# Three sums over partitions: one f32 product with ones, or two fp32r products of a high and a low part

## The chip, the core and the metric

The kernel runs on one core of one Trainium2 chip. The metric is the device time of one execution in microseconds (us), as the median of several runs. An execution is also recorded by the hardware profiler; the engines in the record are PE (TensorE matmuls), PEld (TensorE weight loads), DVE (VectorE), ACT (ScalarE), POOL (GpSimd) and SP (SyncE, which issues all DMAs here). L464 is line 464 of the kernel's file.

## The reference

One transformer block on 2048 tokens of width 512, all in f32. A vector `c` modulates it: six vectors of 512 come out of `silu(c) @ w_mod` and shift, scale and gate two branches.

```python
mod = (_silu(c) @ w_mod).reshape(c.shape[0], 6, 1, -1)
sa, ca, ga, sb, cb, gb = (mod[:, 0], mod[:, 1], mod[:, 2], mod[:, 3], mod[:, 4], mod[:, 5])
h = _layernorm(x, axis=-1) * (1 + ca) + sa
x = x + ga * _A_ref(h, A_wqkv, A_wo)
h = _layernorm(x, axis=-1) * (1 + cb) + sb
x = x + gb * _B_ref(h, B_w_gate, B_w_up, B_w_down)
```

`_A_ref` is linear attention with 32 heads of 16. With phi(t) = (t + 1 where t > 0, else exp(t)) + 1e-6 it takes `kv = sum over tokens of phi(k) v`, `z = sum over tokens of phi(k)`, and `o = phi(q) kv / (phi(q) z + 1e-6)`, and multiplies by `wo`. `_B_ref` is `((x w_gate) * (x w_up)) w_down`.

The change concerns three sums over the 128 partitions: the gates `ga` (vector 2) and `gb` (vector 5) of `mod`, and `z`.

## The kernel before, in words

**Order.** The order of the work is written out by hand (`tc.manual_schedule()`): each engine executes its instructions in the order in which the source issues them, and waits on semaphores for its operands. All working tiles of 128x512 come from one pool of 99 buffers (tag `"t"`); a new tile waits until the last reader of its buffer is done. Products write into PSUM banks: four `bank()`s that are taken in turn, and four `acc_bank()`s.

**Products in parts.** Nearly all matmuls use operands that are split into a high part of type fp32r and a low part that holds the rest. `split` does this: a copy to fp32r on ACT (L183) and a subtraction on DVE (L184), which needs the copy. `product` (L196 to L198) then issues three matmuls: high by high, high by low, low by high.

**The token loop.** The first part of the kernel goes over 16 token tiles of 128 tokens (`for i in range(NT)`). In tile i the source issues, in this order:

1. `proj(i + 2, wk)`, twelve matmuls (L196 to L198) of the normalised tokens by the key weights; in the last tiles the query projections of tiles 4 and 5 instead, of which tile 15 issues that of tile 5.
2. `k_split_x(i + 1)` and `k_split(i + 1)`: the parts of the tokens and of phi(k) for the next tile, on ACT (L183, L318) and DVE (L184, L319).
3. `k_phi`, or in the last tiles `q_a` and `q_b`: two ACT instructions (L291, L292), then one on DVE (L295) that needs them.
4. `z_add(i + 1)`: phi(k) of the next tile added into `zacc` on DVE (L312). After tile 14's, `zacc` holds 128 partial sums per column, one in each partition.
5. In tile 15 only: the product of `zacc` with a 128x128 tile of ones (L464), which sums over the partitions and gives every partition the result, and its copy `zb` on ACT (L466).
6. `t_tile(i, ...)`: twelve matmuls (L327 to L329) that add tokens by phi(k) into the four banks `tacc`.
7. `extra[i]`, a table of side work. Its entries that bear on the change: tile 9 ends the weighted sum `accs[2]` of the four row blocks of `w_mod` (`mod_part(2, 2, 3)`, DVE, L161); tile 11 issues `mod_row(2, accs[2])`; tile 14 issues the last part of `accs[5]` (`mod_part(5, 3)`) and splits the four tiles of `wo` (`wo_s`, four ACT copies L183 and four DVE subtractions L184); tile 15 issues `mod_row(5, accs[5])`.

`mod_row` sums over partitions in the same way as step 5: one f32 product with `ones` (L176) and a copy on ACT (L178).

**After the loop.** `den_z` reduces `zb` on DVE (L480, L481), and `den_a(0, 0, 1)` multiplies and reduces twice (L486, L492, L486, L492). Query projections of tiles 6 and 7 run on PE. `tacc` is scaled on ACT (L535) and shifted by `zb` on DVE (L536), four tiles; these are split (L183 on ACT, L184 on DVE, four each) into `tt`. Then `kvps` is built: for each of four column groups, `product` over k = 0 to 3 of the parts of `wv[k]` and of `tt[k]`, 128x128 matmuls at L196 to L198. The first group already takes all four `tt[k]`, and the second matmul of each three takes the low part of `tt[k]`.

The second half of the kernel (attention output, second norm, and the gated feed-forward in a form with fewer block products, L837 and L916 to L918) is untouched.

## Time and profile before

| | us |
|---|---|
| median of 3 runs | 572.92 (571.94 to 573.11) |
| span of the profiled execution | 570.9 |
| PE busy | 560.6 (98%) |
| PEld busy | 457.3 (80%) |
| DVE busy | 373.8 (65%) |
| ACT busy | 279.7 (49%) |
| POOL busy | 185.6 (33%) |

The span runs from the first to the last recorded instruction of one execution; the runs' times take in what lies around it, 2.0 us between this span and the median. In the timeline view a row gives start, duration, engine, line, operation, tiles and shapes; "x4" means that four instructions of a kind were merged into one row, and a bracket gives the idle time of the engine just ahead and what ended it. An f32 matmul of 128x512 shows as two PE records ("x2"). Ends of matmuls are modelled by the profiler, so PE is read from starts.

### The profile page before, as it was taken

How to read it: one execution, taken by the hardware profiler on the slowest of the kernel's cores; microseconds unless marked ns; L12 is line 12 of the kernel's file. 1: busy time of each engine (PE TensorE's matmuls, PEld its weight loads, DVE VectorE, ACT ScalarE, POOL GpSimd, SP SyncE). 2: the span in 40 equal slices, each digit the busy share in tenths (PEclk: the TensorE clock that was granted, in tenths of full speed). 3: DMA queues.
4: the chain of work that ended last, by engine and by line, in shares of the span. 5: the costliest groups of instructions: out<-in, count | busy, mean ns of one | idle time of the engine just before them, and what ended most of it. 6: DMA issues, size and time to landing. Idle time of an engine off the chain costs nothing.

```text
span 570.9 us, 7343 instructions
## 1 busy us (share of the span) xinstructions
PE 560.6 (98%) x2569; PEld 457.3 (80%) x2569; DVE 373.8 (65%) x613; ACT 279.7 (49%) x500; POOL 185.6 (33%) x191
## 2 busy tenths in 40 slices
PE   7999999999999999999989999999999999999997
PEld 6778888888888778878878888887888888888885
DVE  6876868868768876768776777755554434344444
ACT  3785857546456535445865545533333333334110
POOL 2000000000011300000389666665667446556200
PEclk9999999999999999999999999999999999999999
DMA  8900223302301000804208462699436122100004
GB/s 279 378 6 2 73 75 102 121 0 57 96 0 52 24 1 37 258 0 136 68 2 276 147 209 93 218 337 335 126 110 174 29 56 55 57 18 2 0 1 147
DMA packets 50165, 59.34 MB, mean 104 GB/s; under 512 B 6416, under 2 KB 26896, under 8 KB 50128
## 3 DMA queue, kind: packets, MB, share of 16 engines
q1 hardware_dynamic: 50128, 58.87, 32.0%
q8 instruction: 20, 0.33, 0.2%
q14 instruction: 17, 0.14, 0.1%
HBM read 43.12 MB, written 15.73 MB: 103 GB/s over the span
## 4 chain that ended last, share of the span: by engine, by line
PE 88%; DVE 4%; ACT 2%; DMA 2%; POOL 2%; issue 1%; SPq 0%; POOLq 0%; DVEq 0%; ACTq 0%
PE bank L837 28%; PE acc L614 7%; PE acc L916 6%; PE acc L917 6%; PE acc L918 6%; PE bank L198 5%; PE bank L196 5%; PE bank L197 5%; PE acc L329 3%; PE acc L328 3%; PE acc L327 3%; PE bank L691 2%; PE bank L692 2%; PE bank L690 2%; PE bank L250 1%; PE bank L578 1%
## 5 line engine op out<-in xcount | busy, mean ns | idle before, releaser
L837 PE MATMUL bank<-h,w 128*128 128x512 f32 (+1 forms) x798 | 185.3, 390 | 1.6 <-DVE u L892 1.6
L837 PEld LDWEIGHTS bank<-h,w 128*128 128x128 f32 (+1 forms) x798 | 148.2, 186 | 34.9 <-DVE u L892 2.5
L842 ACT ACTIVATE bank<-bank 128x512 f32<-128x512 f32 (+1 forms) x38 | 22.2, 583 | 144.7 <-PE bank L837 144.7
L677 DVE TENSOR_TENSOR x<-acc,x 128x512 f32<-128x512 f32 x72 | 48.9, 690 | 49.2 <-PE acc L918 48.5
L823 POOL TENSOR_TENSOR w<-raw,w 128x256 fp32r<-128x256 f32 (+3 forms) x38 | 42.2, 1111 | 97.0 <-ACT w L816 76.7
L184 POOL TENSOR_TENSOR w<-raw,w 128x512 fp32r<-128x512 f32 (+1 forms) x25 | 35.5, 1422 | 115.9 <-DVE mv L226 87.5
L916 PE MATMUL acc<-w,kh 128*128 128x512 f32 (+1 forms) x152 | 59.2, 390 | 0.0
L917 PE MATMUL acc<-w,kh 128*128 128x512 f32 (+1 forms) x152 | 59.2, 390 | 0.0
L918 PE MATMUL acc<-w,kl 128*128 128x512 f32 (+1 forms) x152 | 59.1, 389 | 0.0
L234 POOL TENSOR_TENSOR rstd<-ve,half 128x4 f32<-128x4 f32 (+1 forms) x9 | 9.4, 1045 | 138.2 <-DVE ve L233 136.6
L184 DVE TENSOR_TENSOR kl<-u,kh 128x512 fp32r<-128x512 f32 (+1 forms) x38 | 27.4, 761 | 34.5 <-ACT kh L183 32.6
L823 POOL TENSOR_TENSOR w<-t,w 128x512 fp32r<-128x512 f32 (+1 forms) x38 | 48.0, 1286 | 0.0
L196 PE MATMUL bank<-w,h 128*128 128x512 f32 x112 | 44.9, 401 | 0.0
L198 PE MATMUL bank<-w,h 128*128 128x512 f32 x112 | 43.9, 392 | 0.0
L197 PE MATMUL bank<-w,h 128*128 128x512 f32 x112 | 43.6, 389 | 0.0
L614 PE MATMUL acc<-w,xh 128*128 128x512 f32 x120 | 38.1, 398 | 0.0
L916 PEld LDWEIGHTS acc<-w,kh 128*128 128x128 f32 (+1 forms) x152 | 28.5, 188 | 6.0
L918 PEld LDWEIGHTS acc<-w,kl 128*128 128x128 f32 (+1 forms) x152 | 28.5, 188 | 6.0
L917 PEld LDWEIGHTS acc<-w,kh 128*128 128x128 f32 (+1 forms) x152 | 28.5, 188 | 6.0
L243 ACT ACTIVATE n<-x,nmr,rstd 128x512 f32<-128x512 f32 x32 | 24.1, 805 | 17.2 <-DVE nmr L237 17.2
L892 DVE TENSOR_TENSOR u<-bank,u 128x512 f32<-128x512 f32 (+1 forms) x19 | 13.1, 691 | 28.8 <-PE bank L837 28.8
L183 ACT ACTIVATE w<-raw 128x512 fp32r<-128x512 f32 (+2 forms) x44 | 26.4, 618 | 3.2 <-DMA raw<-in_A_wqkv_dram 2.2
(177 smaller groups left out, 1098.1 us busy)
## 6 DMA issues: line engine op xcount, KB each, us to landing
raw<-in_w_mod_dram SPq DMA_DIRECT2D x24, 256.0 KB, 3.7
raw<-in_B_w_down_dram SPq DMA_DIRECT2D x20, 256.0 KB, 3.0
raw<-in_B_w_gate_dram SPq DMA_DIRECT2D x36, 128.0 KB, 3.5
raw<-in_B_w_up_dram SPq DMA_DIRECT2D x36, 128.0 KB, 3.6
x<-in_A_x_dram SPq DMA_DIRECT2D x16, 256.0 KB, 5.4
kept<-f SPq DMA_DIRECT2D x16, 256.0 KB, 2.1
f<-kept SPq DMA_DIRECT2D x16, 256.0 KB, 4.6
side_s<-h SPq DMA_DIRECT2D x16, 256.0 KB, 2.9
```

The costliest lines, as they stand in the source:

```text
L183: nc.scalar.activation(h, src, AF.Copy)
L184: (low or nc.vector).tensor_tensor(l, src, f32(h), op=ALU.subtract)
L196: nc.tensor.matmul(ps, ah, bh, start=i == 0, stop=False)
L197: nc.tensor.matmul(ps, ah, bl, start=False, stop=False)
L198: nc.tensor.matmul(ps, al, bh, start=False, stop=i == n - 1)
L614: nc.tensor.matmul(yps[i], x, y, start=False, stop=k == KD - 1 and x is al, skip_group_check=True)
L677: nc.vector.tensor_tensor(xt, dn[j], xt, op=ALU.add)
L823: sub = lambda out, x, y: (on or nc.gpsimd).tensor_tensor(out, x, f32(y), op=ALU.subtract)
L837: mm = lambda x, y, **kw: nc.tensor.matmul(ps, x[:, k], y, skip_group_check=True, **kw)
L916: nc.tensor.matmul(dn[j], hh[:, a:b], dh[:n], start=i == 0, stop=False)
L917: nc.tensor.matmul(dn[j], hh[:, a:b], dl[:n], start=False, stop=False)
L918: nc.tensor.matmul(dn[j], hl[:, a:b], dh[:n], start=False, stop=i == len(hs) - 1)
```

## The change

The three products with ones take fp32r operands: a second tile of ones is made in fp32r by a copy on POOL at the start, and `column_sums` multiplies it by the high and the low part of the operand, two matmuls into one bank. The operands are split with `split_raw` (one ACT copy, one DVE subtraction, two new tiles of the pool each) a token tile or two ahead of the product: `accs[2]` at the end of tile 9, `zacc` at the head of tile 14's side work, `accs[5]` in tile 14 behind `mod_part(5, 3)` and ahead of the `wo` splits. Nothing else moves in the source; of the copies and subtractions, none of the old ones goes away.

```diff
+    ones_r = consts.tile([P, P], F32R, name="ones_r")
+    nc.gpsimd.tensor_copy(ones_r, ones)
     ps_idle = T(ps_acc, "acc")
...
-    def mod_row(v, acc):
+    def column_sums(pair):
         ps = bank()
-        nc.tensor.matmul(ps, ones, acc, start=True, stop=True)
+        for i, x in enumerate(pair):
+            nc.tensor.matmul(ps, ones_r, x, start=i == 0, stop=i == 1)
+        return ps
+
+    def mod_row(v):
+        ps = column_sums(halves.pop(v))
         t = consts.tile([P, D], F32, name=f"row{v}")
         nc.scalar.activation(t, ps, AF.Copy)
         return t
+
+    halves = {}
...
-             9: lambda: (mod_part(2, 2, 3), mod_load(4)),
+             9: lambda: (mod_part(2, 2, 3), mod_load(4), halves.update({2: split_raw(accs[2])})),
...
-             11: lambda: (mod_part(3, 3), mod_part(4, 0, 1), rows.update({2: mod_row(2, accs[2])})),
+             11: lambda: (mod_part(3, 3), mod_part(4, 0, 1), rows.update({2: mod_row(2)})),
...
-             14: lambda: (mod_part(5, 3), wo_s.extend(split_raw(x) for x in raw_o)), 15: lambda: rows.update({5: mod_row(5, accs[5])})}
+             14: lambda: (halves.update({"z": split_raw(zacc)}), mod_part(5, 3), halves.update({5: split_raw(accs[5])}), wo_s.extend(split_raw(x) for x in raw_o)), 15: lambda: rows.update({5: mod_row(5)})}
...
         if i == NT - 1:
-            zps = bank()
-            nc.tensor.matmul(zps, ones, zacc, start=True, stop=True)
+            zps = column_sums(halves.pop("z"))
```

## The prediction

> **What bounds the kernel now.** First the page's busy times and the list of what PE waited for, over the whole span.

> ```profile
> PE 560.6 (98%) x2569; PEld 457.3 (80%) x2569; DVE 373.8 (65%) x613; ACT 279.7 (49%) x500; POOL 185.6 (33%) x191
> ```
> ```profile
> PE acc L143 <- DVE w L138: 2.0, 1, 2.0
> PE bank L257 <- ACT n L243: 1.6, 1, 1.6
> PE bank L837 <- DVE u L892: 1.6, 2, 1.5
> ```

> PE is the bound: 98% busy, and its three longest waits make 5.2 us of 570.9. So a microsecond taken from PE is gained, unless PE then meets an operand that isn't ready. That has to be looked for behind each of the three products. The timeline of PE around the first of them and at the head of `kvps`:

> ```profile
> 107.30 1.02 PE L176 MATMUL bank<-f,ones 128*128 128x512 f32 x2
> 107.76 0.79 PE L196 MATMUL bank<-w,h 128*128 128x512 f32 x1
> 108.39 0.39 PE L197 MATMUL bank<-w,h 128*128 128x512 f32 x1
> 108.62 0.40 PE L198 MATMUL bank<-w,h 128*128 128x512 f32 x1
> ...
> 139.11 0.22 PE L196 MATMUL bank<-w,w 128*128 128x128 f32 x1
> ...
> 139.95 0.28 PE L198 MATMUL bank<-w,w 128*128 128x128 f32 x1
> 140.06 0.28 PE L196 MATMUL bank<-w,w 128*128 128x128 f32 x1
> 140.24 0.33 PE L197 MATMUL bank<-w,w 128*128 128x128 f32 x1
> 140.40 0.28 PE L198 MATMUL bank<-w,w 128*128 128x128 f32 x1
> ```

> An fp32r matmul of 512 columns follows the one before at 0.23 (108.39 to 108.62). From the f32 product's start to L197 are 1.09; less 0.23 for the L196 between, the product takes 0.86. In `kvps` the starts are 0.11 apart, except into the L197 at 140.24: 0.18. That one takes the low part of `tt[3]`, the last of four subtractions on DVE. Here are DVE and ACT from tile 14 to that point.

> ```profile
> 120.53 1.54 DVE L161 SCALAR_TENSOR_TENSOR f<-raw,sc,f 128x512 f32<-128x512 f32 x2
> ...
> 125.20 0.69 DVE L295 SCALAR_TENSOR_TENSOR h<-bank,h 128x512 f32<-128x512 f32 x1 [1.86 <-ACT h L292]
> 125.81 0.68 DVE L312 TENSOR_TENSOR z<-z,phi 128x512 f32<-128x512 f32 x1
> 126.41 0.74 DVE L161 SCALAR_TENSOR_TENSOR f<-raw,sc,f 128x512 f32<-128x512 f32 x1
> 127.08 2.49 DVE L184 TENSOR_TENSOR w<-raw,w 128x512 fp32r<-128x512 f32 x4
> 130.64 0.69 DVE L295 SCALAR_TENSOR_TENSOR h<-bank,h 128x512 f32<-128x512 f32 x1 [1.08 <-ACT h L292]
> ...
> 134.09 0.69 DVE L492 TENSOR_REDUCE den<-f 128x32 f32<-128x512 f32 x1
> 135.04 2.74 DVE L536 SCALAR_TENSOR_TENSOR n<-zb,col,n 128x512 f32<-128x512 f32 x4 [0.26 <-ACT n L535]
> 137.70 2.49 DVE L184 TENSOR_TENSOR w<-n,w 128x512 fp32r<-128x512 f32 x4
> ```
> ```profile
> 123.91 0.60 ACT L291 ACTIVATE h<-bank 128x512 f32<-128x512 f32 x1 [3.65 <-PE bank L198]
> 124.54 0.63 ACT L292 ACTIVATE h<-h 128x512 f32<-128x512 f32 x1
> 125.08 2.18 ACT L183 ACTIVATE w<-raw 128x512 fp32r<-128x512 f32 x4
> 129.35 0.60 ACT L291 ACTIVATE h<-bank 128x512 f32<-128x512 f32 x1 [2.10 <-PE bank L198]
> 129.98 0.63 ACT L292 ACTIVATE h<-h 128x512 f32<-128x512 f32 x1
> 130.52 0.67 ACT L466 ACTIVATE zb<-bank,eps_z 128x512 f32<-128x512 f32 x1
> 133.83 0.60 ACT L178 ACTIVATE row<-bank 128x512 f32<-128x512 f32 x1 [2.64 <-PE bank L176]
> 134.32 2.42 ACT L535 ACTIVATE n<-acc,col 128x512 f32<-128x512 f32 x4
> ```

> The four lows of `tt` end at 137.70 + 2.49 = 140.19, and PE goes on at 140.24: no slack at all. From 125.20 to 140.19 DVE stands still for only 1.1 (ahead of 130.64) and 0.3 (ahead of 135.04). So in this stretch DVE work beyond about 1.4 us ends on the path.

> **The products.** Two fp32r products should cost 2 x 0.23 = 0.45 in place of 0.86: PE gains 0.41 each, 1.23 for three. The form (512 columns, 128x128 weights) is that of L196 to L198, so I take 0.23; the other end is no gain (0.86). [...]

> **Ones in fp32r.** One POOL instruction of 128x128 more, near 2.6.

> ```profile
> 2.21 0.34 POOL L98 TENSOR_SCALAR_AFFINE_SELECT mask<-mask 128x128 f32<-128x128 f32 x1
> 6.58 0.71 POOL L234 TENSOR_TENSOR rstd<-ve,half 128x2 f32<-128x2 f32 x1 [3.91 <-DVE ve L233]
> ```

> By the nearest row it takes 0.34. POOL then idles 3.91 until DVE's variance comes, and PE reads the tile first at 107. Cost nothing; without that cover the first norm would be 0.34 later.

> **Tile 9's split.** It puts a copy (0.62, below) on ACT ahead of the next tile's copies, and it must wait for DVE's sum.

> ```profile
> 97.32 0.62 ACT L183 ACTIVATE xh<-n 128x512 fp32r<-128x512 f32 x1
> 98.61 0.73 ACT L318 ACTIVATE kh<-phi,eps_phi 128x512 fp32r<-128x512 f32 x1 [0.67 <-DVE phi L295]
> ```
> ```profile
> 105.04 0.39 PE L329 MATMUL acc<-kl,xh 128*128 128x512 f32 x1
> ```
> ```profile
> 99.03 1.53 DVE L161 SCALAR_TENSOR_TENSOR f<-raw,sc,f 128x512 f32<-128x512 f32 x2
> ...
> 118.81 0.69 DVE L295 SCALAR_TENSOR_TENSOR phi<-bank,phi 128x512 f32<-128x512 f32 x1 [2.38 <-ACT phi L292]
> ```

> The sum ends at 100.56, the copy at 101.2. Behind it on ACT wait L183 (now to 101.8 instead of 97.9) and L318 (102.5 at the latest; were it 0.67 later again, 103.1). DVE's last low (L319, 0.68) is then ready by 103.9 at worst, and PE first wants it at 105.04. DVE runs 2 to 3 late in tiles 10 and 11, since ACT's L291 and L292 move too, and catches up where it idles for ACT (2.38 ahead of 118.81). The buffers come free later too, so SP's loads for vector 5 and `wo` are issued up to about that much later, but `wo` (last issue 108.44, 2.8 to land) isn't read before 125.08:

> ```profile
> 104.96 3.85 SPq L110 DMA_DIRECT2D raw<-in_A_wo_dram  x4
> ```
> ```profile
> raw<-in_A_wo_dram SPq DMA_DIRECT2D x4, 256.0 KB, 2.8
> ```

> Cost nothing; the cover is 1.1 us at PE. The product's 0.41 is kept, as PE (first figures of the row below: us, and busy us) has no gap up to tile 14: all that follows PE, up to L291 at 123.91, is 0.41 earlier.

> ```profile
> 108.50:123.50 15.00, 15.00 (x76) 12.57 (x75) 10.45 (x18) 6.54 (x11) 0.00 (x0) 1.00 0.15 53
> ```

> **Tile 14's splits**, the step that decides. Every hand-over costs 0.03 (L292 ends at 125.17, L295 starts at 125.20); a DVE or ACT instruction starts 0.08 to 0.1 before the end of the one ahead when it needs nothing from it. Copies take 0.62 (row at 97.32), subtractions 0.68.

> 1. `z_add` (L312) ends at 126.49 - 0.41 = 126.08.
> 2. The copy of `zacc` on ACT runs from 126.11 to 126.73, its subtraction from 126.76 to 127.44. DVE stands still for 0.68 meanwhile.
> 3. `mod_part(5, 3)` (0.74) ends at 128.10. It isn't run in the gap, although its operands are there since 122.07 (end of the L161 pair): DVE executes in order.
> 4. Copy of `accs[5]`: 128.13 to 128.75; subtraction 128.78 to 129.46, DVE still for another 0.7.
> 5. `wo`: ACT's four copies (2.18) end at 130.83, 3.6 later than now; DVE's four lows (2.49) at 131.87.
> 6. Behind the copies on ACT stand L291 and L292 of the last query tile: end 130.83 - 0.1 + 0.60 + 0.03 + 0.63 = 132.0. L295 on DVE starts at 132.03, 1.39 later than 130.64. `zb` (0.67) is ready at 132.6, just in time for L480.
> 7. Up to the last L492 DVE is packed: its end moves from 134.78 to 136.17. The 0.26 wait and 0.08 overlap before L536 are absorbed (ACT's first L535 is ready by 134.6), so L536 starts at 136.09: 1.05 later.
> 8. The fourth low of `tt` ends at 141.24 instead of 140.19. PE, 1.23 early, waits from 137.9 on in stops that add up to 1.23 + 1.05 = 2.3, and leaves this place **1.05 later than now**.

> The gains of `z` and `accs[5]` thus buy nothing: PE waits longer by the same amount. From there DVE, ACT and PE feed each other with unchanged work, so I expect the lateness to stay. Sum on the profiled span: 570.9 + 1.05 = 571.95; on the median, which lies 2.0 above the span, 572.92 + 1.05 = **574.0**. Bounds: without the 0.41 of the first product (no gain of fp32r) +1.46; with hand-overs of 0.10 each, as from L295's end (98.51) to L318 (98.61), four times, +0.28 more, so +1.7; with hand-overs free, +0.9.

> [...] Could the `wo` work slip into the gaps, DVE would end it by about 130.3, L295 would not be late, and the sum would be 572.5. The row decides it here: the L161 at 126.41 had its operands at 122.07 and stood through the 1.86 idle ahead of 125.20.

> **Rivals.**

> *The gain arrives whole (other side).* Place: the fourth low of `tt`. If it ended by 140.19 - 1.23 = 138.96, PE would lose nothing and the time would be 572.92 - 1.23 = 571.7. It pays off below that point in part; above 140.19 it turns into a loss. For it: DVE idles 1.4 in the stretch. Against: steps 2 and 4 add two subtractions (1.2) and two gaps (1.4), which is more. Chance 0.07.

> *Late, but made up later.* PE's waits ahead of L837 (1.6 in two) could shrink if what ends them were fixed in time; then 572.9 to 573.4. Against: they end with DVE's L892, whose work follows PE. Chance 0.08.

> *The pair isn't cheaper than f32* (the change doesn't do what it says): no 0.41, 572.92 + 1.46 = 574.4. Against: 0.23 for every fp32r row. Chance 0.07.

> *Longer chain*: hand-overs up to 0.10 or copies held up on ACT, 574.3 to 575.2. For it: steps 2 to 6 pass between ACT and DVE five times. Chance 0.12.

> **How the numbers follow.** Forecast 574.0, chance 0.66, own range 573.7 to 574.4. Slower by over 0.2% (about what can be told here) means over 574.07, so the forecast lies on that edge: I give 0.4 of it to slower. Slower: 0.07 + 0.12 + 0.66 x 0.4 = 0.45; same: 0.08 + 0.66 x 0.6 = 0.48; faster 0.07. Range 572.7 to 575.2: it leaves out the whole gain and the far end of the longer chain.

> **What would show it.** In the profile of the changed kernel: fp32r products with 0.23 from start to start and no records of 592 ns at the three products; ACT idle ahead of two copies in tile 14 with DVE named; the four `wo` copies near 128.7; L295 (then L304) near 132.0; four waits of PE for DVE in the first group of `kvps`, 2.3 together, the first the longest; no new wait of PE between 99 and 137. Wrong if PE passes that group without waiting, or if the lateness at 150 is not that at the end.

## The result, and the profile after

| | before | after |
|---|---|---|
| median | 572.43 us (571.85 to 573.11, 4 runs) | 580.47 us (579.20 to 580.63, 4 runs) |
| span of the profiled execution | 570.9 us | 577.5 us |

The changed kernel is slower: 1.0139 times the time before, 95% interval 1.0125 to 1.0152. The forecast was 574.0, with a range up to 575.2. The profiled execution of after is the shortest of the four: it lost 6.6 us of span, and the median run lost 8.0.

The products themselves do what was forecast. PE's timeline of after, around the first of them and at the head of `kvps` (L196 to L198 of before are L205 to L207 now):

```profile
106.81 0.63 PE L179 MATMUL bank<-w,ones_r 128*128 128x512 f32 x2
107.27 0.39 PE L205 MATMUL bank<-w,h 128*128 128x512 f32 x1
107.50 0.39 PE L206 MATMUL bank<-w,h 128*128 128x512 f32 x1
...
137.39 0.22 PE L205 MATMUL bank<-w,w 128*128 128x128 f32 x1
139.02 0.33 PE L206 MATMUL bank<-w,w 128*128 128x128 f32 x1 [1.41 <-DVE w L193]
139.18 0.28 PE L207 MATMUL bank<-w,w 128*128 128x128 f32 x1
139.29 0.28 PE L205 MATMUL bank<-w,w 128*128 128x128 f32 x1
139.62 0.33 PE L206 MATMUL bank<-w,w 128*128 128x128 f32 x1
...
140.82 0.33 PE L206 MATMUL bank<-w,w 128*128 128x128 f32 x1
...
142.22 0.32 PE L206 MATMUL bank<-w,w 128*128 128x128 f32 x1
142.33 0.41 PE L207 MATMUL bank<-w,w 128*128 128x128 f32 x1
142.55 0.42 PE L205 MATMUL bank<-w,w 128*128 128x128 f32 x1
...
152.05 0.63 PE L206 MATMUL bank<-w,h 128*128 128x512 f32 x1
152.47 0.43 PE L207 MATMUL bank<-w,h 128*128 128x512 f32 x1
152.74 0.40 PE L205 MATMUL bank<-w,h 128*128 128x512 f32 x1
```

The pair takes 0.46 (106.81 to 107.27). PE is 0.49 earlier at its start than before (107.30), since this execution's loads came sooner (at 17 us DVE waits 0.25 for a tile of `x`, in before 0.85), and 0.89 earlier at the L206 of 107.50 (before: 108.39). The first stop for DVE, 1.41, stands where it was forecast, and three short ones follow. At 140.82 PE is 0.58 later than before (140.24): 0.58 + 0.49 = 1.07 lost, where 1.05 was forecast.

Then comes what was not forecast. From 142.33 on the 128-column matmuls start 0.21 apart instead of 0.11, and the 512-column ones 0.43 instead of 0.23, until 152.47. PE waits for nothing there. The windows view (us; busy us and instructions of PE, PEld, DVE, ACT and POOL; granted clock; DMA share and GB/s) tells why:

```profile
138.90:142.31 3.41, 3.14 (x22) 2.72 (x23) 3.41 (x7) 2.36 (x5) 0.00 (x0) 1.00 1.03 297
142.31:152.54 10.23, 10.23 (x39) 9.17 (x39) 4.84 (x8) 0.63 (x1) 0.00 (x0) 0.50 0.37 108
152.54:156.00 3.46, 3.46 (x17) 2.83 (x16) 0.69 (x1) 1.23 (x2) 0.00 (x0) 1.00 0.00 0
```

The granted clock is 0.50 for 10.23 us. By the clock records of the trace of after it had been full for 136.53 us (5.77 to 142.30), it was half for 10.24, and full again for 423.25; in before it was full for 563.20 us in one piece. These are 40.0, 3.0, 124.0 and 165.0 times 3.413 us. I take that as the step of the clock in these kernels, an estimate from the four lengths; the shortest half-clock stretch inside any of them is 3.42 (after once more, below). The matmul that starts at 147.10 in before starts at 152.47 in after:

```profile
147.10 0.39 PE L198 MATMUL bank<-w,h 128*128 128x512 f32 x1
```

The lateness of the matmul behind it is 5.42 (before 147.32, after 152.74), 4.84 more than at 140.82. Up to 277 it stays there (5.50), and between 277 and 288 another 1.10 is lost. Here are DVE and POOL at that place, of after and then of before:

```profile
276.53 0.18 DVE L235 BATCH_NORM_AGGREGATE mv<-st 128x2 f32<-128x6 f32 x1
276.96 0.43 DVE L813 TENSOR_TENSOR t<-raw 128x256 f32<-128x256 f32 x1 [0.25 <-DMA raw<-in_B_w_up_dram]
277.43 0.42 DVE L813 TENSOR_TENSOR t<-raw,t 128x256 f32<-128x256 f32 x1
277.77 0.96 DVE L813 TENSOR_TENSOR t<-raw,raw 128x256 f32<-128x256 f32 x1
278.65 1.52 DVE L813 TENSOR_TENSOR t<-raw,t 128x256 f32<-128x256 f32 x1
...
277.55 0.90 POOL L831 TENSOR_TENSOR w<-raw,w 128x256 fp32r<-128x256 f32 x1 [20.30 <-ACT w L824]
278.59 1.30 POOL L831 TENSOR_TENSOR w<-t,w 128x512 fp32r<-128x512 f32 x1
```
```profile
271.03 0.18 DVE L226 BATCH_NORM_AGGREGATE mv<-st 128x2 f32<-128x6 f32 x1
271.13 0.41 DVE L805 TENSOR_TENSOR t<-raw 128x256 f32<-128x256 f32 x1
271.57 0.43 DVE L805 TENSOR_TENSOR t<-raw,t 128x256 f32<-128x256 f32 x1
271.91 0.42 DVE L805 TENSOR_TENSOR t<-raw,raw 128x256 f32<-128x256 f32 x1
272.25 0.96 DVE L805 TENSOR_TENSOR t<-raw,t 128x256 f32<-128x256 f32 x1
...
272.05 0.88 POOL L823 TENSOR_TENSOR w<-raw,w 128x256 fp32r<-128x256 f32 x1 [20.26 <-DMA raw<-in_B_w_up_dram]
272.89 2.73 POOL L823 TENSOR_TENSOR w<-t,w 128x512 fp32r<-128x512 f32 x2
```

Four equal subtractions on DVE start 0.33 later against the instruction ahead of them (0.43 behind its start in after, 0.10 in before), and so two of them, not one, start while one of POOL's runs. Each of these three ends 0.28 behind POOL's: at 273.21 (272.25 + 0.96) behind 272.93 before, at 278.73 behind 278.45 and at 280.17 behind 279.89 after. PE's waits at 283.90 and 294.26 are longer for it. The sum for the profiled execution: -0.49 (start) + 1.07 + 4.84 + 0.08 (small changes up to 277) + 1.10 = 6.60.

### The profile page after: what moved, and what is told of

The parts are those of the page before. It is cut to its first block, busy times and chain, and to the rows that moved or that the text cites. A ratio compares the mean times of both kernels' runs of the same rounds, so it can differ in the third digit from the quotient of the medians.

```text
span 577.5 us, 7352 instructions
## 1 busy us (share of the span) xinstructions
PE 565.2 (98%) x2569; PEld 461.6 (80%) x2569; DVE 376.9 (65%) x616; ACT 281.2 (49%) x503; POOL 185.6 (32%) x192
## 4 chain that ended last, share of the span: by engine, by line
PE 85%; DVE 5%; DMA 4%; POOL 2%; ACT 1%; issue 1%; SPq 1%; POOLq 0%; DVEq 0%; ACTq 0%
PE bank L845 27%; PE acc L924 6%; PE acc L925 6%; PE acc L926 6%; PE acc L622 6%; PE bank L205 5%; PE bank L207 5%; PE bank L206 5%; PE acc L338 3%; PE acc L336 3%; PE acc L337 3%; PE bank L699 2%; PE bank L700 2%; DMA raw<-in_A_wqkv_dram 2%; PE bank L698 2%; PE bank L259 1%
## 5 line engine op out<-in xcount | busy, mean ns | idle before, releaser
L845 PE MATMUL bank<-h,w 128*128 128x512 f32 (+1 forms) x798 | 185.6, 390 | 2.3 <-DVE u L900 2.0
L243 POOL TENSOR_TENSOR rstd<-ve,half 128x4 f32<-128x4 f32 (+1 forms) x9 | 9.4, 1045 | 137.4 <-DVE ve L242 135.5
L205 PE MATMUL bank<-w,h 128*128 128x512 f32 x112 | 45.2, 403 | 0.0
L207 PE MATMUL bank<-w,h 128*128 128x512 f32 x112 | 44.7, 399 | 0.0
L206 PE MATMUL bank<-w,h 128*128 128x512 f32 x112 | 44.6, 398 | 0.0
## 6 DMA issues: line engine op xcount, KB each, us to landing
raw<-in_w_mod_dram SPq DMA_DIRECT2D x24, 256.0 KB, 3.8
raw<-in_B_w_down_dram SPq DMA_DIRECT2D x20, 256.0 KB, 3.0
x<-in_A_x_dram SPq DMA_DIRECT2D x16, 256.0 KB, 5.4
kept<-f SPq DMA_DIRECT2D x16, 256.0 KB, 2.1
f<-kept SPq DMA_DIRECT2D x16, 256.0 KB, 4.6
side_s<-h SPq DMA_DIRECT2D x16, 256.0 KB, 2.8
```

Source lines behind the costliest of these rows:

```text
L205: nc.tensor.matmul(ps, ah, bh, start=i == 0, stop=False)
L206: nc.tensor.matmul(ps, ah, bl, start=False, stop=False)
L207: nc.tensor.matmul(ps, al, bh, start=False, stop=i == n - 1)
L845: mm = lambda x, y, **kw: nc.tensor.matmul(ps, x[:, k], y, skip_group_check=True, **kw)
```

## The experiments

The theories in the expectations turn on one question. Does the loss come from the 1.05 us of lateness and from what DVE, ACT and PE do to each other behind it, or from the clock, which falls when too little streams through PE for a while? The second theory, an estimate of mine, goes on: the clock can change once in each 3.413 us (the step above), by the share of that window in which PE streams columns. I estimate the share as (columns streamed) x 0.213 us / 512 over the window's length, where 0.213 is half of the 0.427 at which 512-column matmuls follow each other at half clock (11 starts from 148.21 to 152.47 in after); this takes all of the 0.427 for streaming. A matmul of 128 columns then streams 0.053, though at full clock the starts are 0.11 apart. So by this count a stop lowers the share, and a run of 128-column matmuls counts as about half a stop. In the expectations, theory G is the second one (W in the eighth, where the window is first named), S says that a long stop by itself brings the clock down, F blames the fp32r products, D the transfers, and N tile 9's split.

Each time given is a median; "before" ran on the same chip with it: at 572.18 for vector 2 alone, tile 14's splits alone, the six matmuls in after, and `wo` in tile 13; at 572.38 for the two kernels once more; at 572.34 for the others.

### Vector 2 alone in parts

`z` and vector 5 stay f32 products; tile 9's split and the pair for `mod_row(2)` remain.

```diff
-             14: lambda: (halves.update({"z": split_raw(zacc)}), mod_part(5, 3), halves.update({5: split_raw(accs[5])}), wo_s.extend(split_raw(x) for x in raw_o)), 15: lambda: rows.update({5: mod_row(5)})}
+             14: lambda: (mod_part(5, 3), wo_s.extend(split_raw(x) for x in raw_o)), 15: lambda: rows.update({5: mod_row(5, accs[5])})}
```

> Only the sum for vector 2 is made in parts (tile 9); z and vector 5 stay f32 products and tile 14 is as before. Theory G (tile 14's splits make PE stop at the head of kvps, and the stops let the granted clock fall to half for about 10 us): no stops beyond those of before, no clock at 0.5 after 100 us, and the 0.41 of one product gained: 0.999 of before, 571.9 to 572.3. Rival F (the fp32r pairs themselves take so much work from PE that the clock falls): a third of the cause is there, and if the clock falls at all it is late in the loop: 573 to 578. Rival N (tile 9's split costs something in tiles 10 and 11 that the prediction put at nothing): 573 or more with a clock of 1.00.

Measured: 571.55 us (571.00 to 572.24, 10 runs), ratio 0.9991 (0.9982 to 1.0000), 0.6 below before. No clock fall in its profile until PE's work ends. That agrees with a gain of 0.41 where nothing waits, though the interval reaches up to no gain, and no cost of tile 9's split can be seen.

### Tile 14's splits alone

The kernel before, with the parts of `zacc` and `accs[5]` made in tile 14 and used by nobody; the three sums stay f32 products.

```diff
-             14: lambda: (mod_part(5, 3), wo_s.extend(split_raw(x) for x in raw_o)), 15: ...
+             14: lambda: (split_raw(zacc), mod_part(5, 3), split_raw(accs[5]), wo_s.extend(split_raw(x) for x in raw_o)), 15: ...
```

> The kernel before with tile 14's two splits added and not used: products stay f32, tile 9 is as before. By the prediction's count DVE is 1.46 us late at the fourth low of tt, and PE, which isn't early here, stops for 1.5 in all (the first stop about 0.2 to 0.4). Theory G in its weak form (any stop of this sum is enough): clock at 0.5 for 10 us, 578 to 581. Theory G in its strong form (it takes the long first stop, which PE's earlier arrival makes): clock 1.00, 572.4 + 1.46 = 573.9. Rival F: f32 products as before, so the clock holds: 573.9 as well; a time near 580 rules F out.

Measured: 578.39 us (573.60 to 578.55, 5 runs), ratio 1.0092 (1.0060 to 1.0125). Here PE isn't early, and its first stop is only 0.58; yet the clock fell. PE's timeline, then the windows view:

```profile
138.50 0.22 PE L196 MATMUL bank<-w,w 128*128 128x128 f32 x1
139.30 0.33 PE L197 MATMUL bank<-w,w 128*128 128x128 f32 x1 [0.58 <-DVE w L184]
```
```profile
138.87:142.28 3.41, 2.83 (x20) 2.41 (x20) 3.41 (x7) 2.67 (x5) 0.00 (x0) 1.00 0.81 229
142.28:152.52 10.24, 10.24 (x40) 9.36 (x40) 5.15 (x9) 0.63 (x1) 0.00 (x0) 0.50 0.38 111
```

One of the five executions, 573.60 us, had a mean clock of 0.999 against 0.990 in the other four: the same kernel without the fall is 4.8 us shorter. That leaves 1.4 us for the late splits, so the larger part of the loss comes with the clock, and it needs neither the products nor a long stop.

### Six unused matmuls ahead of `kvps`

```diff
     kvps = bank()
+    for _ in range(6):
+        nc.tensor.matmul(kvps, wv[0][0][:, :P], wv[0][0], start=True, stop=True)
     for g in range(KD):
```

The six matmuls of 512 columns (6 x 0.227 = 1.36 us) are extra work whose results are overwritten. They were put into after, and for control into before.

> The changed kernel with six more matmuls of 128x512 ahead of kvps' first group, into the bank that the group then overwrites: 1.36 us of PE work that nobody uses, in the place where PE stood still for 1.41. Theory G: PE is busy where it stopped, the clock stays at 1.00, the chain's lateness remains: 572.4 + 1.1 = 573.5, that is 7 us faster than the changed kernel though it has more work. Rival F (the fp32r pairs let the clock fall, not the stops) and rival D (the slowdown from 142 us on is the transfers' doing, 317 GB/s there, the clock only follows): more work of PE at that place changes nothing or adds 1.36: 580.5 to 581.9.

> The kernel before with the same six unused matmuls ahead of kvps' first group. PE has no stop there, so they cost what they take: 6 x 0.227 = 1.36, of which 0.06 comes back at the fourth low: 573.5, clock 1.00. If it came out at 572.2 the fillers would be free wherever they stand, and the run with fillers in the changed kernel would prove nothing about its stop.

Measured (573.5 was expected for each): in after 574.26 us (573.51 to 580.89, 5 runs), ratio 1.0064 (1.0014 to 1.0115); in before 573.22 us (572.80 to 574.42, 10 runs), ratio 1.0020 (1.0011 to 1.0030). More work makes the changed kernel 6.2 us shorter, and the same work makes the kernel before 0.9 longer. In after the stop of 1.41 is gone from the list of waits and the profiled execution has the full clock; in one of the five, 580.89, the clock was 0.988, and in one, 575.02, 0.997. The short stops between the products of the first group remain, and with two of five below the full clock this kernel stands near the edge; the profiled execution also has the loss at 277 that after has.

### `wo` split in tile 13

The four splits of `wo` move one tile ahead, so that ACT and DVE have less ahead of `tt`.

```diff
-             13: lambda: (mod_part(5, 0, 1, 2), cols.update({4: ...})),
-             14: lambda: (..., halves.update({5: split_raw(accs[5])}), wo_s.extend(split_raw(x) for x in raw_o)), ...
+             13: lambda: (mod_part(5, 0, 1, 2), cols.update({4: ...}), wo_s.extend(split_raw(x) for x in raw_o)),
+             14: lambda: (..., halves.update({5: split_raw(accs[5])})), ...
```

> The changed kernel with the four splits of wo issued at the end of tile 13 instead of behind the two new splits in tile 14: ACT idles 3.65 us there and DVE 1.86, so the eight instructions leave the chain that made the lows of tt late. Theory G: the lows come about 0.5 to 1.2 us earlier than before, PE's stops are under 1 us in all, the clock stays at 1.00: 571.2 to 571.9, faster than both kernels. Rival F: all three fp32r pairs are there, the clock falls: 577 to 581. Rival D (transfers): the loads after 137 us come as early or earlier, so 577 to 581 too.

Measured: 571.81 us (571.07 to 576.23, 10 runs), ratio 1.0004 (0.9986 to 1.0023). DVE's row of the lows of `tt` in its profile:

```profile
136.86 2.49 DVE L193 TENSOR_TENSOR w<-n,w 128x512 fp32r<-128x512 f32 x4
```

They start 1.42 sooner than in after (138.28), and the long stop of PE is gone. Eight of ten executions have a clock of 0.999 or 1.0; two, at 574.55 and 576.23 us, have 0.992 and 0.991. So the short stops that are left may still be enough now and then; the profiled execution is one of the eight, and doesn't show where the two lost their time.

### Query products of tile 8 ahead of `kvps`

```diff
     q_tile(7)
+    ps8 = proj(8, wq)
     kvps = bank()
```

The call stands some lines below in after; the work is the same, 2.7 us of it moved (12 x 0.227).

> The changed kernel with the twelve matmuls of proj(8) (2.7 us) moved from behind kvps to ahead of it; all splits and their lateness stay. Theory G: PE comes to kvps near 140.2 and no longer stops for the lows (the last comes near 140.8, wanted near 141.1), the clock stays at 1.00, and PE keeps part of the 1.23 of the three products; DVE's work behind kvps has one projection less to hide under, so some 0.6 goes back: 571.3 to 572.0, against 580.5 of the changed kernel. Rival F (the fp32r pairs let the clock fall): 577 to 581.

Measured: 573.39 us (571.86 to 574.21, 10 runs), ratio 1.0018 (1.0008 to 1.0028). The median misses the expected 571.3 to 572.0, but no execution lost the 5 us. The three at full clock took 571.86 to 572.60; the seven others, 573.26 to 574.21, have clocks of 0.996 to 0.998, which is about one window of half clock (3.413 / 2 = 1.7 us, 0.003 of 572). The profiled execution was one of the full ones, so this experiment doesn't show where that window lies.

### Vector 5 as f32, the other two in parts

```diff
-             14: lambda: (halves.update({"z": split_raw(zacc)}), mod_part(5, 3), halves.update({5: split_raw(accs[5])}), wo_s...
+             14: lambda: (halves.update({"z": split_raw(zacc)}), mod_part(5, 3), wo_s...
```

> The changed kernel without the split of vector 5: z and vector 2 in parts, vector 5 an f32 product. By the prediction's own count the chain of tile 14 then loses steps 3 and 4's copy and subtraction (1.35), and ACT's wo copies end at 128.8 instead of 130.8, before PE's last query projection, so L295 is on time: the lows are no later than before, PE's stops under 1 us, clock 1.00: 571.5 to 572.0. If the split of z alone already makes the lows late, 573 with clock 1.00 or 577 to 580 with the clock at 0.5.

Measured: 571.52 us (571.37 to 572.51, 10 runs), ratio 0.9986 (0.9977 to 0.9996): shorter than both kernels. One copy and one subtraction fewer in the chain of tile 14 remove the long stop, to which PE also comes about 0.4 later, with one f32 product more; no execution's clock was below 0.998. The pair for `z` gains nothing that can be seen here: vector 2 alone took 571.55.

### Unused matmuls behind the stop

Eight matmuls of 384 columns behind the first group of `kvps` in after; extra work again. At 0.213 for 512 columns they are 8 x 0.16 = 1.28 us, an estimate; in the profile 1.46 lie between the start of the first and that of the next product (140.98 to 142.44).

```diff
         product(kvps[:, a:b], [(cut(wv[k], a, b), cut(tt[k], a, b)) for k in range(KD)])
+        for _ in range(8 if g == 0 else 0):
+            nc.tensor.matmul(kvps[:, P:], wv[0][0][:, :P], wv[0][0][:, P:], start=True, stop=True)
```

> The changed kernel with eight unused matmuls of 384 columns behind kvps' first group, so not in PE's stops: those stay as they are (1.4 and three of 0.2). As many columns as the six of 512 ahead of it. Theory W (the clock falls when too few columns stream in one stretch of 3.41 us, whatever the reason; stops and matmuls of 128 columns with 0.11 from start to start both lower it): the stretch from 138.9 to 142.3 gets about 1.2 us of streaming more, the clock holds: 572.2 + 1.1 + 1.4 = 574.7. Theory S (the stop itself, over 1 us long, is what lets it fall): the clock falls as before and the fillers are added, 580.5 to 582.

Measured: 577.08 us (575.63 to 577.65, 4 runs), ratio 1.0088 (1.0071 to 1.0105). The stop stands as in after, and the profiled execution kept the full clock behind it:

```profile
138.90 0.33 PE L206 MATMUL bank<-w,w 128*128 128x128 f32 x1 [1.39 <-DVE w L193]
```
```profile
135.65:139.06 3.41, 2.02 (x11) 1.49 (x10) 3.41 (x6) 2.68 (x5) 0.00 (x0) 1.00 0.17 30
139.06:142.47 3.41, 3.26 (x20) 2.83 (x21) 3.41 (x6) 2.08 (x4) 0.00 (x0) 1.00 1.06 314
```

So here the stop of 1.39 by itself didn't bring the clock down, and neither did the transfers, at 314 GB/s in the second row. Nor does PE's busy time sort the windows: 2.02 of 3.41 here and no fall, 2.83 with tile 14's splits alone and a fall. The time is above the 574.7 that follows from 572.34 + 1.05 + 1.28: the loss at 277 (1.1) makes 575.8, and the three longer executions have clocks of 0.996 to 0.997, by the same arithmetic about one window again.

### The same two kernels once more

After, and the kernel with the matmuls behind the stop, both unaltered, to see an execution with another clock.

> The changed kernel once more, unaltered, for the place of the other half-rate time: its profiled execution had a mean granted clock of 0.99 and a span of 577.5 us, its other executions 0.987 to 0.988 and 578.7 to 578.9. Theory G (the granted clock falls after a window of 3.4 us in which few columns are streamed): a clock of 0.987 is one window of half rate more than 0.99 (3.413 us of half rate take 1.7 us of 579 away, 0.003 of the mean), so in an execution at 0.987 the half rate lasts 13.65 us in all, either four windows in one piece from 142.3 on, or three there and one elsewhere, most likely at 284 to 295, where the next stops stand. Theory S (the stops themselves): the half rate lasts 10.2 us in every execution and the rest of the time, 1.3 us, is longer stops. An execution of 0.99 shows neither.

> The kernel with eight unused products of 384 columns behind the first group of kvps once more, unaltered: its profiled execution had no fall of the clock and a span of 573.9 us, its other executions clocks of 0.996 to 0.999 and times of 575.6 to 577.7 us. Theory G: an execution at 0.997 has one window of half rate (3.4 us, 1.7 us of time), and its place is where a window holds the fewest columns; by my count of columns that is 284 to 295, or 139 to 146. Theory S: no half rate at all, the clock 1.0 as in the execution that I have.

Measured: after took 580.66 us at a clock of 0.988, like its median. The fall at 142 is there as before, and a fourth window lies behind PE's stop of 1.79 at 294:

```profile
292.17:295.58 3.41, 1.62 (x7) 1.05 (x6) 3.27 (x9) 1.18 (x3) 1.73 (x3) 1.00 0.02 5
295.58:299.00 3.42, 3.42 (x9) 2.59 (x8) 1.83 (x3) 0.07 (x1) 3.42 (x3) 0.50 0.00 0
```

Its final lateness is 8.06: 6.70 at 294.36, and 1.36 more by this window. That is the difference between the medians (8.04).

The other kernel took 582.31 us, 6.7 more than in its first profile, with the same stop of PE (1.41 there, 1.39 before) and four windows of half clock in one piece:

```profile
139.54 0.33 PE L206 MATMUL bank<-w,w 128*128 128x128 f32 x1 [1.41 <-DVE w L193]
```
```profile
137.03:140.44 3.41, 1.95 (x12) 1.44 (x10) 3.41 (x6) 3.29 (x6) 0.00 (x0) 1.00 0.40 102
140.44:154.10 13.66, 13.66 (x57) 13.14 (x56) 5.07 (x9) 2.00 (x4) 0.00 (x0) 0.50 0.46 133
```

This is the clearest pair. One kernel, one stop; in one execution a window border (139.06) cuts the slow stretch in two, and nothing falls; in the other the 3.41 us from 137.03 to 140.44 hold the stop and nearly all the 128-column matmuls between the short stops, and the clock falls at their end. My expectation had counted on one window; it took four; by the count below, the first three were not full enough to bring the clock back.

The shares by my count, an estimate from the starts in the traces, of windows that ended with a fall: 0.344 (after, 142.3), 0.295 and 0.369 (after once more, 142.0 and 295.6), 0.297 (tile 14's splits alone), 0.346 (the last kernel). Of the lowest windows without a fall: 0.394 (last kernel, 297.4), 0.399 (tile 8's products first, 287.1), 0.404 (six ahead), 0.420 (after, 295.9). At its end, where PE's work runs out, every kernel's clock falls too, behind windows of at most 0.28. So the border lies between 0.37 and 0.39 by this count, which is good to about one matmul of 128 columns (0.016).

The return can be put in the same measure: in columns, a full-clock window has room for about 8200 (3.413 x 512 / 0.213) and a half-clock one for 4100. The fullest window that ended with a fall held 0.369 x 8200 = 3030; of the half-clock windows the one of 0.72 x 4100 = 2950 was followed by another, and the one of 0.75 x 4100 = 3080 by the full clock (first and last of the four of the last kernel). One border near 3050 columns in 3.413 us, my estimate from these shares, would account for all of these falls and returns; it fits these windows, and was not tested on others.

I count from 20 us on. Ahead of that stand f32 products, and what those stream can't be told from their records (the f32 product at 107.30 of before takes 0.86 for 512 columns, its two records by this count 2 x 0.213); there windows that come out at 0.33 to 0.40 had no fall in nine of the twelve traces (0.335 in after).

If the 3.413 us windows are laid over each trace at every offset, the lowest share that can come out around `kvps` is 0.45 in before, 0.42 with vector 5 as f32, and 0.15 in after; and at 277 to 300 it is 0.45 in the kernels without the loss at 277, and 0.34 to 0.37 in those with it. That agrees with which kernels had a lower clock. With how many executions had it, the agreement is rough. A window under 0.38 comes out around `kvps` at every offset in after, at 0.98 of them with tile 14's splits alone, 0.65 with the matmuls behind the stop, 0.31 with the six ahead, 0.15 with `wo` in tile 13, and at none in before. A mean clock of 0.992 or less, two windows or more, had 5 of 5 executions, 4 of 5, 1 of 5, 1 of 5, 2 of 10, and none of before.

## Why the prediction was wrong

**The products** were right: 0.40, 0.40 and 0.41 gained at the three places. **Ones in fp32r** and **tile 9's split** cost nothing that can be seen, as forecast; vector 2 alone, which has both, gives 0.6 less than before.

**Tile 14's splits**, steps 1 to 8, came out almost row by row. DVE and ACT of after:

```profile
126.29 0.69 DVE L193 TENSOR_TENSOR w<-z,w 128x512 fp32r<-128x512 f32 x1 [0.70 <-ACT w L192]
128.35 0.69 DVE L193 TENSOR_TENSOR w<-f,w 128x512 fp32r<-128x512 f32 x1 [0.70 <-ACT w L192]
...
131.58 0.69 DVE L304 SCALAR_TENSOR_TENSOR h<-bank,h 128x512 f32<-128x512 f32 x1
...
138.28 2.49 DVE L193 TENSOR_TENSOR w<-n,w 128x512 fp32r<-128x512 f32 x4
```
```profile
127.68 0.63 ACT L192 ACTIVATE w<-f 128x512 fp32r<-128x512 f32 x1 [1.42 <-DVE f L163]
128.22 2.18 ACT L192 ACTIVATE w<-raw 128x512 fp32r<-128x512 f32 x4
```

DVE stands still twice for 0.70 (forecast 0.68 and "another 0.7"). L304 starts at 131.58, or 132.07 with the 0.49 of the early start (forecast 132.03). The lows of `tt` end at 140.77, or 141.26 (forecast 141.24). PE's stops add up to 2.30 (from 1.72 early to 0.58 late; forecast 2.3).

The step that failed is the end of step 8: "From there DVE, ACT and PE feed each other with unchanged work, so I expect the lateness to stay." It took a stop as its own length. PE's stops, together with the 128-column matmuls of `kvps` around them, left 3.41 us with 0.344 of streaming by the count above; behind them the clock was half for 10.24 us, and that cost 4.84, more than four times the lateness of 1.07. In after once more a fourth window at 295 costs 1.36 more, and the clocks of three other executions of after (0.987 and 0.988) are those of four windows. None of the rivals had this mechanism; "longer chain", the slowest, ended at 575.2. The test that I named ("if the lateness at 150 is not that at the end") fails too, but the larger error lies ahead of it, between 141 and 153.

The prediction has no term for the clock. Before's profiled execution shows it full from 5.74 to 568.93 of 570.9 us, and nothing there showed what a stop in `kvps` would do to it. In after PE's longest idle stretch ahead of the fall at 142 is 1.41 us, and with tile 14's splits alone it is 0.58. Without the fall, the profiled execution would have lost 6.60 - 4.84 = 1.76 in place of 6.60.

The second miss is smaller: the 1.10 at 277, where "unchanged work" wasn't unchanged in its place against POOL's. The rows at 277 show equal subtractions of DVE take 0.43 and 0.42 where they start ahead of POOL's, and 0.96 and 1.52 where they start beside them; what the two engines share there the rows don't show. Why DVE starts 0.33 late there stays open. The row names a transfer, but the tiles that the subtraction reads had landed by 245.8, 31 us earlier. The delay goes with the kernel and not with the execution: 0.43 to 0.45 from the start of the instruction ahead in all six profiles that have the loss, 0.10 in the six others. The loss stands in the profiles of after (both), six matmuls ahead, tile 8's products first, and matmuls behind the stop (both); it is absent from before, before with six matmuls, vector 2 alone, tile 14's splits alone, `wo` in tile 13, and vector 5 as f32. No experiment was made on it alone.

## What to carry to other kernels

In these runs a stop of PE had two prices: its own length (1.07 us of lateness in after), and its part in a fall of the clock (4.84 us in after), which came where less than about 0.38 of a 3.41 us window was streamed by my count. Where PE runs narrow matmuls (128 columns, 0.11 apart but 0.053 of streaming by that count), the window is half empty already, and there a stop of 1.41 in after, and one of 0.58 with tile 14's splits alone, was followed by the fall; so keep wide matmuls beside it, as moving the products of tile 8 did (7 us less than after with no work taken away). And here a saving on the busiest engine paid only where its operands had slack: the pair for vector 2 pays alone (571.55), the one for `z` adds nothing that can be seen (571.52), and the one for vector 5 turns that into 8 us of loss against before, unless the splits of `wo` make room (571.81).
